# A fused retention and ELU kernel on one core: closing retention outputs pair by pair, loading two chunks earlier, and one multiply on VectorE instead of GpSimd

## The chip, the core and the metric

The kernel runs on one core of a Trainium2 chip. The core has TensorE for matmuls (PE in the profile, with its weight loads as PEld), VectorE (DVE), ScalarE (ACT), GpSimd (POOL), and SyncE (SP), which issues all of this kernel's DMAs in one queue. The metric is the device time of one execution in microseconds (us); lower is better. Everything is float32.

## What is computed

A recurrent retention block feeds a two-layer network. Sizes: batch 4, 8 heads, 768 tokens, head size 64; then 3072 tokens of 512 features, 2048 hidden features, 512 outputs.

```python
# retention: q, k, v are (B, H, S, D) = (4, 8, 768, 64)
gamma = 1.0 - 2.0 ** (-5.0 - np.arange(H))
for t in range(S):
    state = gamma[None, :, None, None] * state + np.einsum('bhd,bhe->bhde', k[:, :, t], v[:, :, t])
    y[:, :, t] = (1 / np.sqrt(D)) * np.einsum('bhd,bhde->bhe', q[:, :, t], state)
x = y.transpose(0, 2, 1, 3).reshape(B * S, H * D)      # (3072, 512)
# network with ELU: w_in is (512, 2048), w_out is (2048, 512)
h = x @ w_in
g = np.where(h > 0.0, h, np.exp(np.minimum(h, 0.0)) - 1.0)
out = g @ w_out
```

## The kernel before

**Tiling.** The 3072 tokens are 24 chunks of 128, numbered 0 to 23, and six groups of 512 tokens (four chunks, `CPB`), numbered `tb` 0 to 5 in the code and called the first to the sixth group in the text. A chunk's q, k and v arrive as one DMA of 1 MB (`load`, L113) into a tile `chunk` of `ldpool`. That pool has four buffers, so chunk m takes the buffer that chunk m - 4 had, and its DMA waits until that chunk is no longer read. After landing, its v is multiplied by powers of gamma (`scale_v`, L293), by GpSimd unless VectorE is asked for.

**Retention of a group** runs on chunks in two pairs (`pp` 0 and 1):
- `scores`: small 64x64 matmuls (L319) into `sc`, masked by VectorE (L330).
- `states`: small matmuls (L359) into `kv`, summed to states by VectorE (L371) or copied by ScalarE (L369).
- `outputs`: a generator for one pair. Its first part does the matmuls inside a chunk (`within`, L415) into two tiles `y` and stops. The second does half of the matmuls with the states (`across`, L430), has VectorE copy a corner of each `y` (`seen`, L399) and stops. The third does the other half of `across`, which waits for the `seen` copies, and then VectorE multiplies both `y` by decay powers into the group's input x (L405). Below, "closing" a pair is this third part. Each pair holds two of the four buffers of the pool `ps_r`.

`outputs_step` spreads this over three visits. In the kernel before, visit 0 starts pair 0, visit 1 starts pair 1, and visit 2 closes both. Between visits TensorE has other matmuls. The first group has its outputs written out by hand and does not use `outputs_step`.

**Network.** Both products are done by Strassen-like schemes with seven products in place of eight, some two levels deep. The first group's first product is plain (`plain_first`, L518 and L542), and its ELU is ScalarE's two steps (L498, L499) and VectorE's L502. While it runs, weights are decoded: ScalarE at L171 to L175, VectorE at L197, L198 and L201. The second product of the second group is `second_twice` (L924): seven outer products `j` in the order 1, 2, 6, 7, 5, 3, 4, each of seven inner products. Each inner product reads one 256 KB weight tile `wq` that SyncE fetches from `scratch_dram` (L830). There are 11 buffers for these, and a fetch is issued in the order of a list as soon as a product gives a buffer back. The first products of the later groups are `big_twice` (L1152), their second products L1248. From the third group on, two groups are done together.

**Order.** The schedule is by hand: generators are advanced step by step, and each engine runs its instructions in the order in which the code issues them. `step` counts the outer products of `second_twice`, and `VISITS` and `LOADS` are tables from a place in that count to a visit or a load. In the kernel before, the third group's visits 0 to 2 are before `step` 1 ends, and the fourth group's four loads follow:

```python
step, VISITS = 0, {(1, "first"): 3, (1, "end"): 4}
LOADS = {(1, "first"): 0, (2, "end"): 1, (5, "end"): 2, (6, "middle"): 3}
```

`retention_step(2, 3)` is visit 1 of the third group and `retention_step(2, 4)` is visit 2. `(1, "first")` is after the first two inner products of the second outer product, `(1, "end")` after its fifth. The fourth group's `scores` begin when `second_twice` ends; its visits lie in the first two products of `big_twice`.

The second group's `scale_v` calls are in the loop over `plain_first`; `n` counts its steps:

```python
if n in (3, 5, 7, 9):
    scale_v(CPB + (n - 3) // 2)
```

Of the kernel before, what the change touches and what calls it, by code (L numbers as in the profile page):

```python
# [19 lines left out]
def kernel(  # L20
# [46 lines left out]
    CPB = TB // C  # L67
# [34 lines left out]
    def load(m, cuts=(0, 2048), behind=None):  # L102

        if m >= NCHUNK:
            return
        t = ldpool.tile([P, 2048], FP32, name="chunk", tag="chunk")
        raw[m] = (
            t[:, 0:1024].rearrange("p (a h c) -> p a h c", a=2, c=C),
            t[:, 1024:2048].rearrange("p (a h d) -> p a h d", a=2, d=D),
        )  # L110
        hold(t, behind)
        for lo, hi in itertools.pairwise(cuts):
            nc.sync.dma_start(t[:, lo:hi], qkv[m, :, lo:hi])  # L113
# [171 lines left out]
    held = {}  # L285

    def scale_v(m, by_vector=False):
        if m >= NCHUNK:
            return
        i = chunks[m][1]  # L290
        v = raw[m][1][:, 0]
        eng = nc.vector if by_vector or m < 2 else nc.gpsimd
        eng.tensor_tensor(  # L293
            out=v, in0=v, in1=vf[:, i].unsqueeze(2).to_broadcast([C, H, D]), op=ALU.mult
        )
# [77 lines left out]
    def states(tb, pp):  # L373

        kvs = [ps_r.tile([P, 2, HP, D], FP32, name="kv", tag="r") for _ in range(2)]
        for x in range(2):
            state_products(kvs, tb, pp, x, range(2))
        for x in range(2):
            for sub in range(2):
                state_sum(kvs, tb, pp, x, sub)  # L380
# [4 lines left out]
    def outputs(tb, pp):  # L385

        y = [ps_r.tile([P, 2 * 2, 2, D], FP32, name="y", tag="r") for _ in range(2)]
        for x in range(2):
            for j in range(4):
                pt = raw[tb * CPB + 2 * pp + j // 2][0][:, 1].rearrange("p h c -> p (h c)")  # L390
                within(tb, pp, x, j, y, lambda p: pt[:, (x * HP + p) * D :][:, 0:D])
        for other in range(2):
            if not other:
                yield
            else:

                for sub in range(2):
                    seen = epool.tile([P, 8], FP32, name="seen", tag="seen")
                    nc.vector.tensor_copy(seen.rearrange("p (j x) -> p j x", x=2), y[sub][:, :, :, 0])  # L399
                yield  # L400
            for x in range(2):
                across(tb, pp, x, other, y)
        i = chunks[tb * CPB + 2 * pp][1]
        for sub in range(2):
            nc.vector.tensor_tensor(  # L405
                out=place_of(x_of(tb)[:, :, 2 * pp * C : 2 * (pp + 1) * C])[:, :, :, sub, :], in0=y[sub],
                in1=place_of(powers[:, :, i * C : (i + 2) * C])[:, :, :, sub, :], op=ALU.mult,
            )

    def within(tb, pp, x, j, y, pt):  # L410
        kv = raw[tb * CPB + 2 * pp + x][1]
        a, u = divmod(j, 2)
        for sub in range(2):
            for c in range(2):
                nc.tensor.matmul(  # L415
                    y[sub][rows(c), j, x, :], lhsT=kv[rows(sub), 0, head(a, u, c), :], rhs=pt(2 * u + c)[rows(sub)],
                    start=(x == 0 and j == 0), stop=False, skip_group_check=True,
                )

    def across(tb, pp, x, other, y):  # L420
        q = raw[tb * CPB + 2 * pp + x][0]
        for u in range(2):
            for a in range(2):
                sub = a ^ other
                n = 4 * pp + 2 * x + sub
                if fresh(tb, n):
                    continue
                for c in range(2):
                    p = 2 * u + c
                    nc.tensor.matmul(  # L430
                        y[sub][rows(c), 2 * a + u, x, :], lhsT=state(tb, n)[rows(a), p, :],
                        rhs=q[rows(a), 0, p, rows(sub)], start=False, stop=True, skip_group_check=True,
                    )

    def outputs_of_first():

        y = [bank(x).rearrange("p a (b x d) -> p (a b) x d", b=2, x=2) for x in "bd"]
        for x in range(2):
            for j in range(4):
                pt = raw[x][0][:, 1].rearrange("p h c -> p (h c)")  # L440
                within(0, 0, x, j, y, lambda p: pt[:, ((j // 2) * HP + p) * D :][:, 0:D])
            yield
            across(0, 0, x, 0, y)
            for sub in range(2):
                if not fresh(0, 2 * x + sub):
                    seen = epool.tile([P, 8], FP32, name="seen", tag="seen")
                    nc.vector.tensor_copy(seen[:, 0:4], y[sub][:, :, x, 0])
            if x:
                yield
            across(0, 0, x, 1, y)  # L450
            if x:
                yield
            for sub in range(2):
                nc.vector.tensor_tensor(
                    out=place_of(xb[:, :, 0 : 2 * C])[:, :, x, sub, :], in0=y[sub][:, :, x],
                    in1=place_of(powers[:, :, 0 : 2 * C])[:, :, x, sub, :], op=ALU.mult,
                )
            if not x:
                yield

    def outputs_step(tb, step):

        if step == 0:
            held["y"] = [outputs(tb, pp) for pp in range(2)]
        if step < 2:
            next(held["y"][step])
            next(held["y"][step])
        else:
            for g in held["y"]:
                next(g, None)  # L470

    half = [slice(0, TH), slice(TH, TB)]

# [83 lines left out]
    def inputs_of_first(f, slots):  # L557

        b11, b12, b21, b22 = (of_first(r, f, t) for r in range(2) for t in range(2))
        t3, t2, t4_ = slots  # L560
        tt = lambda o, x, y: nc.vector.tensor_tensor(out=o, in0=x, in1=y, op=ALU.subtract)
        tt(t3, b22, b12)
        tt(b12, b12, b11)
        yield
        tt(t2, b22, b12)
        tt(t4_, b21, t2)
        for x in range(2):
            inputs[f + x] = {
                1: of_first(0, f + x, 0, 1), 2: of_first(1, f + x, 0, 1), 3: of_first(1, f + x, 1, 1),
                4: t4_[:, x], 5: of_first(0, f + x, 1, 1), 6: t2[:, x], 7: t3[:, x],  # L570
            }
        yield
# [831 lines left out]
    y = outputs_of_first()  # L1404
# [40 lines left out]
    y = outputs(0, 1)  # L1445
# [9 lines left out]
    def run(steps):  # L1455
        for _ in steps:
            pass

    def next_piece(by_vector=False):
        decode_all()  # L1460
        prepare(by_vector=by_vector)
# [8 lines left out]
    for n, _ in enumerate(inner):  # L1470
        if n in (0, 2, 4):
            load(CPB + n // 2)
        if n == 4:
            load(CPB + 3)
        if n in (1, 2, 4, 5, 7, 9):
            next_piece(n in (1, 2, 5, 7))
        if n in (3, 5, 7, 9):
            scale_v(CPB + (n - 3) // 2)
        if n == 4:
            run(inputs_of_first(0, [hslot() for _ in range(3)]))  # L1480
        elif n == 10:
            scores(1, 0)
            scores(1, 1)
        elif n == 11:
            states(1, 0)
            states(1, 1)
            next_piece()
            parts = sums_of_pieces(0)
            next(parts)
        elif n == 12:  # L1490
            outputs_step(1, 0)
            run(parts)
            next_piece()
        elif n == 13:
            outputs_step(1, 1)
            smalls = small_of_pieces(0)
            some(smalls, 3)
        elif n == 14:
            outputs_step(1, 2)
            some(smalls, 2)  # L1500
            decode_all()
        elif n == 15:
            run(smalls)
# [114 lines left out]
    flush()  # L1618
    retention_step(2, 2)
    step, VISITS = 0, {(1, "first"): 3, (1, "end"): 4}  # L1620
    LOADS = {(1, "first"): 0, (2, "end"): 1, (5, "end"): 2, (6, "middle"): 3}
    for s in sec:
        if s == "first":
            step += 1
# [1 line left out]
        if at in VISITS:  # L1626
            retention_step(2, VISITS[at])
        if at in LOADS:
            load(3 * CPB + LOADS[at])
            scale_v(3 * CPB + LOADS[at])  # L1630
        if s == ORDER2[-1]:
# [10 lines left out]
    for nb in range(NB):  # L1642
# [173 lines left out]
        step = 0  # L1816
# [3 lines left out]
        ]  # L1820
        LOADS = [(3, "middle"), (3, "end"), (4, "first"), (4, "middle")]
        for s in sec:
# [4 lines left out]
            if more and at in VISITS:  # L1827
                n = VISITS.index(at)
                retention_step(groups[n // 5], n % 5)
            if more and at in LOADS:  # L1830
                bring(groups[1], LOADS.index(at))
            if s == BIG2[-1]:
# [56 lines left out]
```

## Time and profile before

| what | value |
|---|---|
| runs | 621.24 us median of 3 (621.15 to 623.93) |
| profiled execution | span 621.4 us, from its first to its last instruction; the profile shows no time outside it |
| TensorE | 611.4 us busy (98%), granted clock 1.000 |
| VectorE | 496.7 us busy (80%) |
| ScalarE | 261.0 us busy (42%) |
| GpSimd | 21.2 us busy (3%) |
| DMA | 125.14 MB, mean 201 GB/s |

The table gives the median of the runs and the profile of one execution. "Busy" is the union of an engine's instructions. Matmuls are pipelined and their recorded ends are modelled, so the distance between two starts tells more of TensorE than an instruction's length. In a row of the timeline, the numbers are the start, the length, the engine, the line, the operation, the tiles (out<-in), the shape and the count; a bracket at the end gives the idle time before it and what ended it. "issue" means that the engine waited for nothing that the profile shows. `SPq` is SyncE's queue. In a row of waits the numbers are the total, the times and the longest. In a row by stretches they are the stretch and its length, the busy time and instructions of PE, PEld, DVE, ACT and POOL, the granted clock, the share of DMA and its GB/s.

### The profile page before, as it was taken

How to read it: one execution, taken by the hardware profiler on the slowest of the kernel's cores; microseconds unless marked ns; L12 is line 12 of the kernel's file. 1: busy time of each engine (PE TensorE's matmuls, PEld its weight loads, DVE VectorE, ACT ScalarE, POOL GpSimd, SP SyncE). 2: the span in 40 equal slices, each digit the busy share in tenths (PEclk: the TensorE clock that was granted, in tenths of full speed). 3: DMA queues.
4: the chain of work that ended last, by engine and by line, in shares of the span. 5: the costliest groups of instructions: out<-in, count | busy, mean ns of one | idle time of the engine just before them, and what ended most of it. 6: DMA issues, size and time to landing. Idle time of an engine off the chain costs nothing.

```text
span 621.4 us, 13415 instructions
## 1 busy us (share of the span) xinstructions
PE 611.4 (98%) x5446; PEld 480.9 (77%) x5446; DVE 496.7 (80%) x776; ACT 261.0 (42%) x446; POOL 21.2 (3%) x30
## 2 busy tenths in 40 slices
PE   8999999999999999999999999999999999999998
PEld 6764568888889998888545888888888744788886
DVE  5768889989889875677888987898546897888885
ACT  5888844205542111236898210100144798511110
POOL 2011000000000001000010000110000000000000
PEclk9999999999999999999999999999999999999999
DMA  8697569789575898786811445873654523356453
GB/s 295 285 374 303 174 205 269 235 242 274 204 234 151 301 374 310 231 250 199 274 49 67 122 134 154 268 275 108 206 159 143 151 69 93 118 148 187 153 150 117
DMA packets 79278, 125.14 MB, mean 201 GB/s; under 512 B 6128, under 2 KB 46832, under 8 KB 74480
## 3 DMA queue, kind: packets, MB, share of 16 engines
q1 hardware_dynamic: 79216, 124.28, 62.1%
q8 instruction: 43, 0.70, 0.4%
q14 instruction: 19, 0.16, 0.1%
HBM read 94.63 MB, written 29.62 MB: 200 GB/s over the span
## 4 chain that ended last, share of the span: by engine, by line
PE 86%; DVE 4%; DMA 3%; ACT 3%; issue 2%; SPq 0%; DVEq 0%
PE pa L1248 15%; PE pa L1152 9%; PE pd L1248 8%; PE pa L1199 6%; PE pd L1152 4%; PE pa L765 4%; PE pd L1199 4%; PE pb L1248 4%; PE x L632 3%; DMA wq<-scratch_dram 2%; PE pa L924 2%; PE pa L542 2%; PE pb L1152 2%; PE pa L632 2%; PE pb L1199 2%; PE y L415 2%
## 5 line engine op out<-in xcount | busy, mean ns | idle before, releaser
L1256 ACT COPY ms<-pa 128x256 f32<-128x256 f32 x41 | 15.3, 372 | 108.5 <-PE pa L1248 105.5
L1248 PE MATMUL pa<-gC,wq 128*128 128x256 f32 x224 | 53.1, 381 | 0.0
L1248 PEld LDWEIGHTS pa<-gC,wq 128*128 128x128 f32 x224 | 42.1, 190 | 6.8 <-DVE gT L1216 0.5
L1215 ACT ACTIVATE r<-r 128x512 f32<-128x512 f32 x64 | 40.3, 630 | 2.0
L1163 ACT COPY m<-pa 128x512 f32<-128x512 f32 x32 | 18.7, 585 | 48.9 <-PE pa L1152 48.8
L293 POOL TENSOR_TENSOR chunk<-chunk,vf 128x512 f32<-128x512 f32 x16 | 18.0, 1124 | 381.3 <-DMA chunk<-in_qkv_dram 201.1
L1260 DVE TENSOR_TENSOR res<-pd,ms 128x256 f32<-128x256 f32 x26 | 11.0, 422 | 25.0 <-PE pd L1248 14.1
L1152 PE MATMUL pa<-ts,wq 128*128 128x256 f32 x104 | 26.9, 384 | 0.0
L1248 PE MATMUL pa<-ts,wq 128*128 128x256 f32 x112 | 26.8, 382 | 0.0
L1248 PE MATMUL pd<-w_all,wq 128*128 128x256 f32 x112 | 26.6, 380 | 0.1
L171 ACT ACTIVATE w_all<-wraw 128x1024 uint32<-128x1024 uint32 (+1 forms) x19 | 19.2, 1008 | 16.9 <-PE x L632 9.0
L1248 PE MATMUL pd<-ts,wq 128*128 128x256 f32 x104 | 24.7, 380 | 0.2 <-DVE ts L894 0.2
L1230 DVE TENSOR_TENSOR gC<-w_all,gC 128x1024 f32<-128x1024 f32 x20 | 24.2, 1260 | 0.0
L1248 PEld LDWEIGHTS pd<-w_all,wq 128*128 128x128 f32 x112 | 21.2, 190 | 3.4 <-DVE w_all L894 0.6
L1248 PEld LDWEIGHTS pa<-ts,wq 128*128 128x128 f32 x112 | 21.0, 190 | 2.9
L1248 PE MATMUL pa<-w_all,wq 128*128 128x256 f32 x96 | 22.9, 381 | 0.0
L173 ACT ACTIVATE w_all<-wraw 128x1024 fp8e4<-128x1024 f32 (+1 forms) x19 | 22.6, 1189 | 0.6
L1152 PEld LDWEIGHTS pa<-ts,wq 128*128 128x128 f32 x104 | 19.3, 190 | 4.5 <-ACT m L1163 0.8
L1216 DVE SCALAR_TENSOR_TENSOR w_all<-r,w_all 128x512 f32<-128x512 f32 x32 | 22.0, 688 | 0.7 <-ACT r L1215 0.6
L1248 PEld LDWEIGHTS pd<-ts,wq 128*128 128x128 f32 x104 | 19.7, 190 | 3.2 <-DVE ts L894 0.6
L1199 PE MATMUL pa<-ts,wq 128*128 128x512 f32 x48 | 22.1, 592 | 0.0
L1199 PE MATMUL pa<-gC,w_all 128*128 128x512 f32 x48 | 22.1, 592 | 0.0
(327 smaller groups left out, 1458.0 us busy)
## 6 DMA issues: line engine op xcount, KB each, us to landing
wq<-scratch_dram SPq DMA_DIRECT2D x191, 256.0 KB, 3.2
chunk<-in_qkv_dram SPq DMA_DIRECT2D x22, 1024.0 KB, 7.6
wraw<-in_w_dram SPq DMA_DIRECT2D x15, 1024.0 KB, 7.1
out_dram<-res SPq DMA_DIRECT2D x7, 512.0 KB, 3.3
scratch_dram<-gT SPq DMA_DIRECT2D x12, 256.0 KB, 4.3
wq<-scratch_dram SPq DMA_DIRECT2D x24, 128.0 KB, 3.1
scratch_dram<-w_all SPq DMA_DIRECT2D x12, 256.0 KB, 3.4
scratch_dram<-w_all SPq DMA_DIRECT2D x24, 128.0 KB, 3.2
```

Source lines behind the costliest of these rows:

```text
L171: nc.scalar.activation(flat, lo, AF.Copy, scale=2.0**-29)
L173: nc.scalar.activation(top, hi.bitcast(FP32), AF.Copy, scale=2.0**-120, saturate=False)
L293: eng.tensor_tensor(out=v, in0=v, in1=vf[:, i].unsqueeze(2).to_broadcast([C, H, D]), op=ALU.mult)
L632: nc.tensor.matmul(X[j][:, d, :], lhsT=w[j][:, d * P : d * P + P], rhs=x[j], start=(n == 0 and d == 0), stop=at_end, skip_group_check=True,)
L765: nc.tensor.matmul(ps[:, fi, :], lhsT=w[:, fi, j2, :], rhs=x[:, j2, :], start=(begin and fi == 0 and j2 == 0), stop=(j2 == 1), skip_group_ ...
L1152: nc.tensor.matmul(ps[:, f, :], lhsT=w[:, f, :], rhs=big_xs[j][k], start=(begin and f == 0), stop=True, skip_group_check=True,)
L1163: nc.scalar.copy(o, ps)
L1199: nc.tensor.matmul(ps, lhsT=w[:, k, :], rhs=layer_x[j][:, k], start=False, stop=(k == 1), skip_group_check=True,)
L1215: nc.scalar.activation(r, r, AF.Exp, scale=-1.0)
L1216: return lambda: nc.vector.scalar_tensor_tensor(g, r, -1.0, g, ALU.add, ALU.max)
L1230: nc.vector.tensor_tensor(out=quarter(to, r, t), in0=quarter(x, r, t), in1=quarter(y, r, t), op=op)
L1248: nc.tensor.matmul(ps, lhsT=w[:, f, :], rhs=ts[j][k][:, f // 2, f % 2, :], start=(begin and f == 0), stop=(f == 3), skip_group_check=True,)
```

## The change

Three edits:
- In `outputs_step`, groups with `tb` up to 3 close pair 0 at the head of visit 1, and pair 1 at visit 2. Groups 4 and 5 close both at visit 2, as before. Since group 0 does not come here, groups 1, 2 and 3 change.
- The v of chunk 6 is multiplied by VectorE at step `n` = 8 of `plain_first`, not by GpSimd at step 7.
- The third and the fourth load of the fourth group (chunks 14 and 15) are issued one place sooner each in the count: at `(4, "end")` and `(5, "end")`.

```diff
         if step == 0:
             held["y"] = [outputs(tb, pp) for pp in range(2)]
+        early_end = tb <= 3
+        if step and early_end:
+            next(held["y"][step - 1], None)
+        elif step == 2:
+            for g in held["y"]:
+                next(g, None)
         if step < 2:
             next(held["y"][step])
             next(held["y"][step])
-        else:
-            for g in held["y"]:
-                next(g, None)
...
-        if n in (3, 5, 7, 9):
+        if n == 8:
+            scale_v(CPB + 2, True)
+        if n in (3, 5, 9):
             scale_v(CPB + (n - 3) // 2)
...
-    LOADS = {(1, "first"): 0, (2, "end"): 1, (5, "end"): 2, (6, "middle"): 3}
+    LOADS = {(1, "first"): 0, (2, "end"): 1, (4, "end"): 2, (5, "end"): 3}
```

On the engines, by the order of instructions: TensorE has the same matmuls, with pair 0's closing ones ahead of pair 1's first. On VectorE two L405 move ahead of the second pair's two `seen` copies in each of the three groups, and one L293 is added between the L502 of `pb` and that of `pd`. GpSimd has 15 L293 in place of 16. ScalarE's order does not change. On SyncE chunk 14 comes four `wq`, one output and three `wq` earlier, and chunk 15 three `wq` and one output earlier.

## The prediction

> **What bounds the kernel now.** I read the page first (busy shares, then the chain that ended last), then TensorE's waits, then the timeline around each wait.
>
> ```profile
> PE 611.4 (98%) x5446; PEld 480.9 (77%) x5446; DVE 496.7 (80%) x776; ACT 261.0 (42%) x446; POOL 21.2 (3%) x30
> PE 86%; DVE 4%; DMA 3%; ACT 3%; issue 2%; SPq 0%; DVEq 0%
> q8 instruction: 43, 0.70, 0.4%
> ```
>
> TensorE is busy 98% of the span and carries 86% of the chain, at a granted clock of 1.0 throughout. The change adds and removes no matmul, so it can only pay or cost where TensorE stands still. Those places, from the waits of TensorE:
>
> ```profile
> PE pa L924 <- DMA wq<-scratch_dram: 1.3, 1, 1.3
> PE sc L319 <- issue: 0.6, 1, 0.6
> PE y L415 <- issue: 0.8, 2, 0.5
> PE pa L542 <- DVE gC L502: 0.4, 1, 0.4
> ```
>
> Four holes lie near the edits: 0.4 us at L542 (group one's tail, where one v changes engine), 1.3 us at L924 (group two's second product, while the fourth group's chunks load), and two "issue" holes, at L319 and at the second of the two L415 waits (fourth group's retention). The timeline, by start and length, shows each hole and its neighbour:
>
> ```profile
> 49.05 3.60 PE L542 MATMUL pd<-xb,w_all 128*128 128x512 f32 x8
> 53.05 1.13 PE L542 MATMUL pa<-xb,w_all 128*128 128x512 f32 x2 [0.40 <-DVE gC L502]
> ...
> 218.71 1.06 PE L924 MATMUL pd<-ts,wq 128*128 128x128 f32 x8
> 221.02 1.13 PE L924 MATMUL pa<-ts,wq 128*128 128x128 f32 x8 [1.25 <-DMA wq<-scratch_dram]
> ...
> 245.14 1.04 PE L319 MATMUL sc<-chunk 64*64 64x64 f32 x55
> 246.79 0.35 PE L319 MATMUL sc<-chunk 64*64 64x64 f32 x9 [0.62 <-issue]
> 246.96 1.26 PE L359 MATMUL kv<-chunk 64*64 64x64 f32 x64
> ```
>
> Ends of matmuls are modelled, so I price a hole from start to start against an undisturbed group of the same kind. L542: eight take 3.43 (45.62 to 49.05), here 49.05 to 53.05 is 4.00: 0.57 us. L924: eight take 0.89 (217.82 to 218.71), here 2.31: 1.42 us. L319: 64 small matmuls take 0.98 (191.68 to 192.66), here 245.14 to 246.96 is 1.82: 0.84 us. L415: 250.07 to 251.56 is 1.49 against 0.98: 0.51 us. Together 3.34 us. Nothing else within reach of the edits stands still by more than 0.22 us (L924 at 190.59), so a gain over about 3.6 us is excluded.
>
> **One v on VectorE.** The release of L542 at 53.05 leads to VectorE, and from there to GpSimd:
>
> ```profile
> 50.27 1.04 POOL L293 TENSOR_TENSOR chunk<-chunk,vf 128x512 f32<-128x512 f32 x1 [3.89 <-DMA chunk<-in_qkv_dram]
> ...
> 50.35 2.05 DVE L201 CUSTOM_DVE_ANT_0 w_all<-wraw,w_all 128x2048 uint16<-128x2048 uint16 x1
> 52.32 1.27 DVE L502 SCALAR_TENSOR_TENSOR gC<-r,pa 128x512 f32<-128x512 f32 x2
> ...
> 54.96 1.23 DVE L201 CUSTOM_DVE_ANT_0 w_all<-wraw,w_all 128x2048 uint16<-128x2048 uint16 x1
> ...
> 58.70 0.69 DVE L502 SCALAR_TENSOR_TENSOR gC<-r,pd 128x512 f32<-128x512 f32 x1 [1.92 <-ACT r L499]
> ```
>
> The same L201 takes 1.23 us alone and 2.05 beside GpSimd's multiply: 0.82 lost, which is what makes L502, and so L542, late. It is chunk 6 that is scaled at 50.27; that is the one moved. L201 then ends near 51.6, the r it waits for is there (ScalarE ends it at 51.51), the first L502 ends near 52.2, before the 52.48 at which TensorE could start. Gain 0.57. The multiply itself goes between the L502 of pb and that of pd, where VectorE idles 1.92 us; a two-input 128x512 operation there takes 0.69 (L561, 48.42). It is hidden; without that cover it costs at most 0.69. The chunk landed by 50.3, so VectorE does not wait on it. GpSimd's next multiply (52.58) waits for its own chunk anyway.
>
> The Trainium skill ("Perfetto Trace Analysis", section "Optimizing Scalar/DVE Operations") says the reverse of this edit: where VectorE is saturated, move work off it, even to GpSimd; though it warns in the same place that the two share a port. The stretch agrees with the warning (2.05 against 1.23); by the first half alone this term would be a loss, the fourth case below.
>
> **Outputs pair by pair.** Group one does not go through this routine, so groups two to four change. In each, the 32 closing matmuls of pair 0 (as the trace counts them) move from the third visit to the head of the second. Visits stay three per group, so the price of switching between big and small matmuls stays: zero on TensorE. A switch shows as 0.10 us (193.24 to 194.23, right after small matmuls, against 0.89), so 0.2 up or down per group bounds it. On VectorE two of the four L405 (four take 2.48 at 204.15, so 0.62 each) move ahead of the two "seen" copies, which pair 1's closing matmuls wait for. Group three: seen now starts at 199.67, would end near 201.2, and is wanted at 202.33: 1.1 us spare. In groups two and four VectorE idles before the same copies (0.70 at 78.19, 1.92 at 256.61). Should that cover be gone, up to 1.3 us per group; I take 0.
>
> The use is elsewhere. Load 12 takes the buffer of chunk 8, last read by pair 0's closing matmuls. SyncE issues in order, and stood behind that wait:
>
> ```profile
> SPq L113 <- PE y L430: 4.9, 1, 4.9
> ...
> 201.00:205.00 4.00, 4.00 (x91) 3.81 (x90) 3.06 (x7) 0.53 (x2) 0.00 (x0) 1.00 0.23 43
> 222.00:230.00 8.00, 8.00 (x74) 8.00 (x73) 5.32 (x11) 1.32 (x5) 0.00 (x0) 1.00 1.04 378
> ```
>
> (First the wait in SyncE's queue; then stretches, whose last two columns are DMA share and GB/s.) From 198.4 to 203.1 SyncE issued nothing: DMA fell to 43 GB/s, then had chunk 12, the waiting wq and chunk 13 at once and ran full until past 230. The hole at 221 is a wq that SyncE issued at 213.80, behind chunk 13. Now pair 0 closes near 198.5, so load 12 and the wq behind it go 4.6 us sooner. Full rate 378 GB/s less what the products draw (262 KB per 0.89 us, 294) leaves 84 GB/s to catch up. Serving 4.6 us sooner is 1.7 MB at full rate; the hole of 1.42 us is 0.5 MB. Gain 1.42, bounds 0 and 1.42.
>
> **Two loads sooner.** Chunks 14 and 15 move from 231.25 and 236.29 to about 223.5 and 230. In SyncE's queue they pass four wq, an output and three wq, and then three wq and an output: each passed issue is 0.4 us later, and about 2.8 us behind a chunk's megabyte (1.05 MB at 378). A wq is issued when one of 11 buffers comes free, so 11 x 0.89 = 9.8 us before use; usual landing is 5.5 us in this stretch. The spare 4.3 us covers 2.8. Their buffers (chunks 10 and 11) are long free; GpSimd multiplies both sooner, with nothing queued behind. Cost 0.
>
> What it gives: chunk 15 no longer fills DMA in 236 to 244 (349 GB/s in 236 to 242, 285 in 242 to 250). The "issue" hole stands in the middle of 64 equal matmuls with no semaphore, and small matmuls eat instructions fastest (64 of them with their 64 weight loads in 0.98 us); I read it as instructions arriving late through busy DMA engines. Gain 0.84, bounds 0 and 0.84. The L415 hole follows 4 us later, when scratch stores fill DMA, and those stay: I take 0, bounds 0 and 0.51. In return, fetches near 199 to 203 now meet chunk 12: 0, up to 0.84 by the nearest row.
>
> The Trainium skill ("Runtime: NRT & Kernel Launch", section "Instruction fetch mechanics") tells of instructions streamed in 16 KiB blocks of 256, mostly hidden. The page's row agrees on the size (0.70 MB in 43); by "mostly hidden" the hole has another cause and stays, the third case.
>
> **Sum.** Profiled execution: span 621.4, nothing shown around it, 0.2 above the median of 621.24, so I subtract from the median: 0.57 + 1.42 + 0.84 = 2.83, 618.4 us.
>
> **Cases.** 0.5% of 621.24 is 3.1 us (about what a measurement of this kernel can tell from no change), so the faster side begins at 618.1.
> 1. Three holes close, the L415 one stays: 618.4. Chance 0.38.
> 2. All four close: 621.24 - 3.34 = 617.9. For it: with 0.6 us gained just before, TensorE reaches this L415 earlier against the stores. Chance 0.32.
> 3. Both "issue" holes stay, since they come from how dense the small matmuls are: 621.24 - 1.99 = 619.25. For it: a like hole at 25.4, long before these loads. Against: dense stretches at 60 and 171 have none. Chance 0.10.
> 4. The v is in VectorE's way: + 0.69 - 1.42 - 0.84, 619.7. Against: the 1.92 idle. Chance 0.05.
> 5. The wq hole only moves, and only the v helps: 620.7. Chance 0.06.
> 6. Slower: the two loads come before the backlog is served. Catching up one chunk at 84 GB/s takes 12.5 us, and chunks now stand 11.5, 13.5 and 6.5 us apart. If wq land over 9.8 us after issue from 223 on, each load stalls TensorE its 2.8 us and no DMA hole closes: 621.24 - 0.57 + 5.6 = 626.3. Against: the 6.5 us follow only after most of this product's wq are issued. Chance 0.09.
>
> Faster by over 0.5%: most of case 2 and, 618.4 being 0.3 from the edge, under half of case 1: 0.45. Within: 0.46. Slower: case 6, 0.09. The range leaves out case 6 and reaches from 617.3 (case 2, the 0.22 at 190.59 and 0.4 of switches) to 620.9.
>
> **What would show it.** L201 near 50 takes 1.23 and no idle stands before L542; an L293 on DVE lies between two L502. SyncE's wait on L430 falls under 1 us, DMA in 201 to 205 is busy, no L924 waits for wq. L319 of the fourth group runs its 64 unbroken. I am wrong if L924 or L1152 waits for wq after 223, if L430 waits for "seen", or if a new "issue" hole appears near 200.

## The result and the profile after

| kernel | median (lowest to highest), us | runs | span of the profiled execution |
|---|---|---|---|
| before | 622.67 (620.76 to 624.97) | 22 | 621.4 |
| changed | 620.52 (619.32 to 623.74) | 22 | 618.6 |

The changed kernel takes 0.9973 of the time of before, with a 95% interval of 0.9961 to 0.9985: 0.27% faster, which on 622.67 is 1.7 us (0.9 to 2.4). The medians lie 2.15 apart, the means of the same runs 1.8. Single runs of either kernel scatter with a standard deviation of 1.1 to 1.2 us, so three runs, as the prediction had them, or one profile, say little about 1.7 us.

The page after, rows of its first and fourth parts:

```profile
PE 610.7 (99%) x5446; PEld 481.2 (78%) x5446; DVE 494.7 (80%) x777; ACT 261.0 (42%) x446; POOL 22.1 (4%) x29
PE 89%; DMA 5%; DVE 3%; ACT 1%; SPq 1%; issue 1%; DVEq 0%
```

The matmuls are the same 5446, and their share of the chain grew from 86 to 89%: TensorE does the same work and stands still less. VectorE has one instruction more and GpSimd one less, as the edit says.

TensorE's waits after; the three numbers are the total, the times and the longest:

```profile
PE y L415 <- issue: 0.6, 1, 0.6
PE pd L430 <- DVE seen L447: 0.5, 2, 0.3
PE pa L927 <- DMA wq<-scratch_dram: 0.3, 1, 0.3
PE y L430 <- DVE seen L399: 0.3, 1, 0.3
```

From line 471 on, three lines were added, so the L924 of before is L927 here, L542 is L545 and L502 is L505. Of the four holes that the prediction priced, three are gone, and the `wq` one is down from 1.3 to 0.3. The "issue" wait that is left is the one of the start (at 25.46), which before had too. The waits for `seen` stand as they were, so closing pair 0 early cost nothing here.

The two rows of the fourth group's retention that were broken by an "issue" wait before (L319 at 246.79, L415 at 251.26) run their 64 matmuls through:

```profile
243.27 1.16 PE L319 MATMUL sc<-chunk 64*64 64x64 f32 x64
...
247.32 1.16 PE L415 MATMUL y<-chunk 64*64 64x64 f32 x64
```

SyncE's queue in before, at load 12:

```profile
203.09 0.33 SPq L113 DMA_DIRECT2D chunk<-in_qkv_dram  x1
203.47 4.14 SPq L830 DMA_DIRECT2D wq<-scratch_dram  x7
```

The queue after (its wait on L430, then its timeline), and the stretch in which before had moved 43 GB/s with the next one (the last two columns are DMA share and GB/s):

```profile
SPq L113 <- PE y L430: 0.6, 2, 0.3
```

```profile
197.77 0.33 SPq L113 DMA_DIRECT2D chunk<-in_qkv_dram  x1
200.23 6.50 SPq L833 DMA_DIRECT2D wq<-scratch_dram  x7
207.53 0.34 SPq L968 DMA_DIRECT2D out_dram<-res  x1
207.96 1.81 SPq L833 DMA_DIRECT2D wq<-scratch_dram  x3
209.82 0.42 SPq L113 DMA_DIRECT2D chunk<-in_qkv_dram  x1
```

```profile
201.00:205.00 4.00, 4.00 (x63) 3.81 (x63) 3.78 (x8) 0.53 (x2) 0.00 (x0) 1.00 0.93 347
205.00:213.00 8.00, 8.00 (x74) 8.00 (x73) 4.46 (x11) 1.32 (x5) 1.04 (x1) 1.00 0.82 254
```

The wait of 4.9 us is gone. Load 12 goes out at 197.77 in place of 203.09. The seven `wq` behind it begin at 200.23 in place of 203.47. TensorE is 0.9 us further on in this profile, so the load gains 4.4 us and the `wq` 2.4; the prediction gave 4.6 to both. The quiet stretch runs at 347 GB/s.

VectorE and GpSimd around 50 us after, by start and length:

```profile
50.14 1.23 DVE L201 CUSTOM_DVE_ANT_0 w_all<-wraw,w_all 128x2048 uint16<-128x2048 uint16 x1
50.72 1.55 POOL L293 TENSOR_TENSOR chunk<-chunk,vf 128x512 f32<-128x512 f32 x1 [6.42 <-DMA chunk<-in_qkv_dram]
51.29 1.27 DVE L505 SCALAR_TENSOR_TENSOR gC<-r,pa 128x512 f32<-128x512 f32 x2
...
55.08 0.68 DVE L505 SCALAR_TENSOR_TENSOR gC<-r,pb 128x512 f32<-128x512 f32 x1
...
55.68 0.68 DVE L293 TENSOR_TENSOR chunk<-chunk,vf 128x512 f32<-128x512 f32 x1
```

L201 takes its 1.23 as forecast, and the moved multiply takes 0.68 in VectorE's idle time. But GpSimd still multiplies beside an L201. This is now chunk 7's multiply, whose chunk landed at 50.56, and GpSimd is the one that takes longer, 1.55 in place of 1.04. What decides is in the experiments.

### The profile page after: what moved, and what is told of

Same layout as the page of the kernel before. It is cut to its first block, busy times and chain, and to the rows that moved or that the text cites. A ratio compares the mean times of both kernels' runs of the same rounds, so it can differ in the third digit from the quotient of the medians.

```text
span 618.6 us, 13412 instructions
## 1 busy us (share of the span) xinstructions
PE 610.7 (99%) x5446; PEld 481.2 (78%) x5446; DVE 494.7 (80%) x777; ACT 261.0 (42%) x446; POOL 22.1 (4%) x29
## 4 chain that ended last, share of the span: by engine, by line
PE 89%; DMA 5%; DVE 3%; ACT 1%; SPq 1%; issue 1%; DVEq 0%
PE pa L1251 15%; PE pa L1155 9%; PE pd L1251 8%; PE pa L1202 6%; PE pd L1155 4%; PE pd L1202 4%; PE pb L1251 4%; PE pa L545 3%; PE x L635 3%; DMA wq<-scratch_dram 3%; PE pa L768 3%; PE pa L927 3%; PE pb L1155 2%; PE pa L635 2%; PE pb L1202 2%; PE y L415 2%
## 5 line engine op out<-in xcount | busy, mean ns | idle before, releaser
L293 POOL TENSOR_TENSOR chunk<-chunk,vf 128x512 f32<-128x512 f32 x15 | 19.0, 1265 | 377.2 <-DMA chunk<-in_qkv_dram 201.2
```

The source lines that it names most:

```text
L293: eng.tensor_tensor(out=v, in0=v, in1=vf[:, i].unsqueeze(2).to_broadcast([C, H, D]), op=ALU.mult)
```

## The experiments

**The theories.** T1: the prediction's own, the v gives 0.57, the earlier closing 1.42, the two loads 0.84. T2: some of these holes differ from execution to execution, and a part of the 3.34 us belongs to the one profile shown and not to the kernel. To see that, before and the changed kernel were profiled again as well. Each ratio is against runs of before on the same chip.

**The v alone.**

```diff
-        if n in (3, 5, 7, 9):
+        if n == 8:
+            scale_v(CPB + 2, True)
+        if n in (3, 5, 9):
             scale_v(CPB + (n - 3) // 2)
```

> The kernel before with one edit: chunk 6's v goes to VectorE. Theory A (each edit closes its own hole, and hole sizes are the same in every execution): L201 near 50 takes 1.23 us, the 0.57 us at L542 is gone, the wq hole near 221 stays at about 1.4 us and both issue holes stay; time 0.6 us under before (ratio 0.9991). Theory B (the holes that hang on DMA differ from one execution to the next, and the profile of before was one large draw): the L542 hole is gone in the same way, since nothing of it hangs on DMA, and the time is also 0.6 under before, but the wq hole and the issue holes in this profile have other sizes than 1.42, 0.84 and 0.51. Theory C (the v is in VectorE's way): 0.7 us slower.

Measured: 622.18, ratio 1.0002 (0.998 to 1.0025). The v alone gives nothing that 12 runs show. The interval reaches to a gain of 1.2 us, so for the 0.57 this does not decide alone; the profiles below do.

The trace shows a cost that the prediction had not looked for, behind the last matmul. From its start to the end of the span it is 3.93 us here, and 3.46 to 3.47 in the four profiles of before. The first of GpSimd's two `DRAIN` instructions at the end of the program starts 3.29 us after that matmul in place of 2.96, and takes 0.22 in place of 0.08; the last instructions of all engines come later by as much. All seven profiles of kernels with this v on VectorE have 3.93 to 3.96 there, and all seven with it on GpSimd 3.46 or 3.47. So the edit costs 0.49 us at the end. Why GpSimd is late there is not shown.

**The closing alone.**

```diff
+        early_end = tb <= 3
+        if step and early_end:
+            next(held["y"][step - 1], None)
+        elif step == 2:
+            for g in held["y"]:
+                next(g, None)
```

> The kernel before with one edit: pair 0 closes at the head of the second visit in groups two to four. Theory A: SyncE's wait on L430 is under 1 us, the wq hole near 221 closes (1.42 us), the L542 hole and the issue holes stay: 1.4 us under before (0.9977). Theory B: the wq hole is smaller but not surely gone; the mean gain is under 1.4 us, between 0.3 and 1.2. A rival (the visits themselves cost): switches or seen waits show on L430, time equal or slower.

Measured: 621.62, ratio 0.998 (0.9963 to 0.9998). Load 12's wait on L430 is 0.3, TensorE waits for no `wq`, and by chance this execution shows what the v was about. VectorE and GpSimd in it:

```profile
49.79 1.04 POOL L293 TENSOR_TENSOR chunk<-chunk,vf 128x512 f32<-128x512 f32 x1 [4.99 <-DMA chunk<-in_qkv_dram]
49.91 1.47 DVE L198 TENSOR_SCALAR wraw<-wraw 128x1024 uint32<-128x1024 uint32 x1
51.42 1.23 DVE L201 CUSTOM_DVE_ANT_0 w_all<-wraw,w_all 128x2048 uint16<-128x2048 uint16 x1
```

GpSimd began first, and VectorE's L198, 0.70 elsewhere, took 1.47; TensorE then stood 0.50 us longer at L545.

**The loads alone.**

```diff
-    LOADS = {(1, "first"): 0, (2, "end"): 1, (5, "end"): 2, (6, "middle"): 3}
+    LOADS = {(1, "first"): 0, (2, "end"): 1, (4, "end"): 2, (5, "end"): 3}
```

> The kernel before with one edit: chunks 14 and 15 are loaded one place sooner each. SyncE still stands 4.9 us behind load 12. Theory A: the wq hole near 221 stays at 1.4 us; the issue hole at L319 closes (0.84 us), the one at L415 closes too (0.51, as in the profile of the changed kernel): 0.8 to 1.35 us under before (0.9978 to 0.9987). Theory B: the same holes, with a mean gain under that. A rival (loads before the backlog is served): new wq holes at L924 near 225 to 232, up to 2.8 us per load, time slower by up to 5.6 us.

Measured: 621.04, ratio 0.9969 (0.9955 to 0.9983), the clearest single gain. No "issue" hole at L319 or L415 is left. SyncE's wait is still 4.9 us, and the `wq` holes are still there:

```profile
213.85 1.13 PE L924 MATMUL pd<-ts,wq 128*128 128x128 f32 x8 [0.65 <-DMA wq<-scratch_dram]
...
220.96 1.13 PE L924 MATMUL pa<-ts,wq 128*128 128x128 f32 x8 [1.51 <-DMA wq<-scratch_dram]
```

After 223, where the sixth case of the prediction had put its stalls, nothing waits for a `wq`.

**Before again.** No edit.

> The kernel before, unchanged. Theory A: its profile shows the four holes with the sizes of the first profile: 0.57, 1.42, 0.84 and 0.51 us, span 621.4. Theory B: 0.57 again to within 0.05, but the wq hole and the issue holes differ by half a microsecond or more, and the span with them (the runs of before reach from 620.8 to 625.0 us). The ratio to before is 1.000 either way and shows how far a comparison of this many rounds can be trusted.

Measured: 622.65, ratio 0.9998 (0.9982 to 1.0014). Its profile of the same kernel has other holes. VectorE and GpSimd in it:

```profile
49.91 1.24 DVE L201 CUSTOM_DVE_ANT_0 w_all<-wraw,w_all 128x2048 uint16<-128x2048 uint16 x1
50.18 1.86 POOL L293 TENSOR_TENSOR chunk<-chunk,vf 128x512 f32<-128x512 f32 x1 [3.51 <-DMA chunk<-in_qkv_dram]
```

In the profile shown to the prediction GpSimd began at 50.27 and VectorE 0.08 us later; here VectorE began 0.27 us ahead. Whichever begins first keeps its time, the other waits: 1.86 for GpSimd here, 2.05 for VectorE there. The Trainium skill ("SBUF — State Buffer", section "SBUF: two separate sides") states this as a rule: the two share a port pair, and the one that starts first holds it for the whole instruction. These rows agree.

The fourth group's small matmuls in the same profile (TensorE's timeline):

```profile
243.95 1.04 PE L319 MATMUL sc<-chunk 64*64 64x64 f32 x55
245.86 0.35 PE L319 MATMUL sc<-chunk 64*64 64x64 f32 x9 [0.88 <-issue]
246.03 1.26 PE L359 MATMUL kv<-chunk 64*64 64x64 f32 x64
247.22 1.13 PE L1152 MATMUL pa<-xt,w_all 128*128 128x256 f32 x4
248.19 1.03 PE L1152 MATMUL pd<-ts,w_all 128*128 128x256 f32 x4
249.15 0.92 PE L415 MATMUL y<-chunk 64*64 64x64 f32 x46
250.88 0.50 PE L415 MATMUL y<-chunk 64*64 64x64 f32 x18 [0.81 <-issue]
```

The break comes after the 55th matmul of L319, as in the first profile of before, and then after the 46th of L415, again as there. From the first break to the second there are 9 + 64 + 4 + 4 + 46 = 127 matmuls, as many weight loads and, in the trace, two semaphore instructions: 256. This holds for every "issue" wait of TensorE. The 14 profiles of this document show 18, of 0.17 to 0.88 us, and counted from the start of the program each comes after 193 or 194 instructions more than a multiple of 256. The Trainium skill ("Runtime: NRT & Kernel Launch", section "Instruction fetch mechanics") has instructions come in blocks of 256. The trace agrees.

The trace also has the packets of the instruction queue, `q8`: 43 of 16 KB in each profile, as many as there are such places. The first packet comes after the first place, so I pair each packet with the place after (the trace does not name what a packet holds). Then no place in any of the 14 profiles is passed less than 1.25 us after its packet has ended, and all 18 holes end 1.25 to 1.51 us after it. So at these holes TensorE waits for instructions that arrive late.

**The closing and the loads, v on GpSimd.** The changed kernel with this undone:

```diff
-        if n == 8:
-            scale_v(CPB + 2, True)
-        if n in (3, 5, 9):
+        if n in (3, 5, 7, 9):
             scale_v(CPB + (n - 3) // 2)
```

> The changed kernel with chunk 6's v given back to GpSimd. Theory A (v is worth 0.57 us in every execution): 0.6 us slower than the changed kernel, ratio to before 0.9982. Theory B' (GpSimd and VectorE take turns at a shared port, and whichever starts first goes through; the 0.57 us came up only because GpSimd started 0.08 us before L201 in that one execution): no measurable difference from the changed kernel, ratio near 0.997; in the profile the later one of L293 and L201 is the long one.

Measured: 620.48, ratio 0.9975 (0.9959 to 0.9991). On the same chip the changed kernel has 0.9972. The v is worth nothing that shows.

**The changed kernel again.** No edit.

> The changed kernel, unchanged. If holes have fixed sizes (theory A): span 618.6 again, a wq hole of 0.44 us near 219, no issue hole at L319 or L415, ratio to before 0.9955. If one profile is a single draw (theory B): the wq hole and the start-up differ by up to 1 us and the span with them, and the ratio is again near 0.997.

Measured: 620.35, ratio 0.9972 (0.9954 to 0.999), on another chip, beside 0.9973 in the first comparison. None of the four holes is in its profile (span 617.7).

**Chunk 13's load later.** The changed kernel, with

```diff
-    LOADS = {(1, "first"): 0, (2, "end"): 1, (4, "end"): 2, (5, "end"): 3}
+    LOADS = {(1, "first"): 0, (3, "first"): 1, (4, "end"): 2, (5, "end"): 3}
```

> The changed kernel with chunk 13's load moved from the end of the second step to the first place of the third, about 3 us later. If the wq hole near 219 is made by wq that stand behind chunk 13: it closes (0.44 us in the profile of the changed kernel), ratio to before near 0.996. Rival (the backlog is what counts, not the place): a hole of 0.5 to 1.5 us at L924 shows 2 to 4 us later, near 222 to 226, and the ratio is 0.997 to 0.999.

Measured: 619.66 (619.0 to 620.5), ratio 0.9966 (0.9954 to 0.9978), the lowest median of all kernels. In the first profile of the changed kernel the `wq` issued right behind load 13, at 210.34, landed at 219.02, and the 0.3 us hole that is left ends at 219.16. Here load 13 goes out at 212.51 in place of 209.82, more `wq` pass it, and TensorE stands still for none. It is faster than before; from the changed kernel on the same chip (620.35) its interval does not separate it.

**Pair by pair in all groups.** The changed kernel, with

```diff
-        early_end = tb <= 3
+        early_end = True
```

> The changed kernel with pair 0 closed early in the fifth and sixth groups too. Their outputs lie between 366 and 445, where no hole over 0.15 us stands in TensorE's timeline and DMA is under 300 GB/s. Theory A and B alike: nothing to gain, ratio as the changed kernel, 0.997. Rival: the early L405 delay VectorE there and a wait on ts or res shows at L1251 (0.3 to 1.3 us), ratio near 0.999.

Measured: 624.17, ratio 1.0041 (1.0023 to 1.0059): slower than before. TensorE's waits, and then the timeline where the longest of them falls:

```profile
PE y L430 <- DVE seen L399: 2.7, 3, 2.0
```

```profile
375.47 1.23 DVE L897 TENSOR_TENSOR gC<-gC,gC 128x1024 f32<-128x1024 f32 x1
376.61 0.23 DVE L399 COPY seen<-y 128x8 f32<-128x8 f32 x2
...
376.90 0.27 PE L430 MATMUL y<-chunk 64*64 64x64 f32 x2 [2.00 <-DVE seen L399]
```

Closing pair 0 one visit sooner also needs its `seen` copy one visit sooner. In the fifth group that copy is queued on VectorE behind additions over 1024 columns (L897), and TensorE stands for 2.0 us; a second hole, 0.44, follows at 433.37. Start to start the two cost 2.16 and 0.60. This is the wait that the prediction named for L430, priced at up to 1.3 per group; where VectorE is full it is larger. In groups two to four it did not come. The profiled execution (622.25) is the fastest of this kernel's twelve runs, so the others lose more than these two holes; where is not shown.

**Pair by pair in the third group alone.** The changed kernel, with

```diff
-        early_end = tb <= 3
+        early_end = tb == 2
```

> The changed kernel with the early closing kept in the third group alone (the one whose chunk 8 load 12 waits for); groups two and four close both pairs at the third visit again. If all that the early closing brings is load 12: the same as the changed kernel, ratio near 0.997, SyncE's wait on L430 under 1 us, no wq hole over 0.5 us. Rival (the earlier L405 in groups two and four matter as well): ratio nearer 1.000, and a wait on L405 or a y buffer shows in TensorE's timeline near 83 to 87 or 256 to 260.

Measured: 620.91, ratio 0.9977 (0.9961 to 0.9992): not to be told from the changed kernel. The second and fourth groups add nothing that shows. Its profile holds a miss for the theory. SyncE's wait is 0.3 here too, and yet (TensorE's timeline):

```profile
220.40 1.13 PE L927 MATMUL pa<-ts,wq 128*128 128x128 f32 x8 [1.74 <-DMA wq<-scratch_dram]
```

**Three more profiles**, one execution each: two of before and one of the changed kernel, to see how the holes scatter.

> The kernel before, for its profile alone. Holes of fixed size: 0.57, 1.42, 0.84 and 0.51 us. Holes that differ by execution: the L542 hole is there only if GpSimd's L293 starts before VectorE's L201; the wq hole lies between 1.0 and 1.7, the L319 hole between 0 and 1.1, the L415 hole between 0.4 and 1.1.

> As the run before it: the kernel before, a further execution. The sum of the four holes over all profiles of this kernel, less what the changed kernel keeps, should come near the 1.7 us that the runs show, not the 2.8 of the first pair of profiles.

> The changed kernel, for its profile alone: wq hole between 0 and 1 us, no L542 hole, no issue hole at L319, at most 0.5 us at L415.

Measured: 622.75 and 622.66 for before, 620.70 for the changed kernel. In us that TensorE loses, start to start as in the prediction, a hole being the time over that of an undisturbed group:

| profile | L542 (v) | `wq` | L319 | L415 | sum |
|---|---|---|---|---|---|
| before, as predicted from | 0.57 | 1.42 | 0.84 | 0.51 | 3.34 |
| before, second | 0 | 1.21 | 1.09 | 1.03 | 3.33 |
| before, third | 0 | 1.80 | 0.28 | 0 | 2.08 |
| before, fourth | 0 | 1.52 | 0.54 | 1.03 | 3.09 |
| v alone | 0 | 1.48 | 0 | 0.49 | 1.97 |
| closing alone | 0.50 | 0 | 0 | 0.41 | 0.91 |
| loads alone | 0 | 2.50 | 0 | 0 | 2.50 |
| changed, first | 0 | 0.44 | 0 | 0 | 0.44 |
| changed, second | 0 | 0 | 0 | 0 | 0 |
| changed, third | 0 | 0.64 | 0 | 0 | 0.64 |
| closing and loads | 0 | 0.40 | 0 | 0 | 0.40 |
| load 13 later | 0 | 0 | 0 | 0 | 0 |
| all groups | 0 | 0 | 0 | 0 | 0 |
| third group alone | 0 | 1.90 | 0 | 0 | 1.90 |

(All groups has its two holes at L430 beside these.) The third profile of the changed kernel has a new hole as well:

```profile
203.24 0.60 PE L927 MATMUL pa<-gC,wq 128*128 128x128 f32 x4 [0.34 <-issue]
```

It is the "issue" hole near 200 that the prediction had allowed for, 0.51 start to start; it shows in one of three profiles of the changed kernel, and it too stands at a place of the 256.

## Why the prediction was right or wrong

**Direction and range held, the size did not.** Forecast was 618.4, in a range of 617.3 to 620.9; measured is 620.52. The three terms made 2.83 us; the runs give 1.7 (0.9 to 2.4). Faster, but within 0.5%.

**The v: the term that failed.** The prediction gave it a gain of 0.57 and no cost. The 0.57 was a price from one execution. In it GpSimd began 0.08 us ahead of VectorE. In the other three profiles of before VectorE began first, GpSimd waited, and TensorE lost nothing. A hole that comes in one profile of four is worth 0.14 on average (0.15 over all seven profiles with this v on GpSimd, two of which have it). The prediction took from the row that the multiply slows L201, and did not ask which of the two comes first in another execution. The multiply itself was hidden, as said, and the fourth case, in which it costs 0.69 in VectorE's way, did not come. But the premise that the change "can only pay or cost where TensorE stands still" left out what follows the last matmul, and there the edit costs 0.49. By the profiles the term is thus a loss of about 0.35 in place of a gain of 0.57. The runs (1.0002, and 0.9975 against 0.9972) show neither; their intervals are wider than that.

**The closing: right, at its upper bound.** SyncE's longest wait on L430 at a load went from 4.9 to 0.3 or less in each of the eight profiles of kernels that close the third group's pair 0 early. In the six profiles that close late the `wq` holes sum to 1.2 or more, 1.66 on average. In the eight that close early the average is 0.42, and four of those have none. So the term of 1.42 measured 1.2. It is a lower chance of a hole and not its end: 0.44 and 0.64 in two profiles of the changed kernel, and 1.90 in the one with the third group alone. "Gain 1.42" was the upper bound taken as the value. Cost 0 held in the groups that were changed, and the fifth and sixth, which were left out, show what it is without cover.

**The loads: right, and more than priced.** In the six profiles with the loads late (four of before, v alone, closing alone) the L319 hole is there four times and the L415 hole five times; in the eight with the loads early neither is ever there. The sum took L319 at 0.84, and L415 at 0 since the scratch stores stay. On average before loses 0.69 at L319 and 0.64 at L415, and both go: that step was too careful, and it was the second case that came. That the holes come from instructions that arrive late is shown by their places and by the packets. With the loads late, the packet ended 1.25 to 1.51 us before TensorE passed the place in eleven of the twelve cases (six profiles, L319 and L415); with the loads early, 1.66 to 2.27 us before in all sixteen. What differs between the two is when chunk 15 lands. In the six profiles it was still landing 1.45 to 2.60 us after TensorE had passed the place before L319's; in the eight it had landed at least 0.86 us before that. The twelfth case, 2.19 at L319 with the closing alone, shows that a packet can come through beside the load, so that the load's bytes hold the packet up is likely but not shown. The third case is out, in which these holes come from how dense the small matmuls are: they reach 0.88 us of idle time, and they go when two loads move. The Trainium skill ("Runtime: NRT & Kernel Launch", section "Instruction fetch mechanics") calls the cost of a new block mostly hidden. In 584 of the 602 places of these 14 traces no wait shows, which agrees; the 18 waits do not.

**The base: wrong.** "Nothing shown around it, 0.2 above the median" set a span beside a run's time. The profiled execution of the changed kernel has a span of 618.6 and took 620.36, and the second one of before 621.7 and 623.47: some 1.8 us lie outside the span, in every run for which both are on record (1.72 to 1.85). The profiled execution of before thus took about 623.2 (an estimate, 621.4 + 1.8), and the 621.24 from which the sum was subtracted was 1.4 below the median of 22 runs. From 622.67, the two terms that held, 1.42 + 0.84, give 620.4. That this is 0.1 from the measured 620.52 is partly luck, since the closing was priced too large, and what was left out goes both ways: 0.64 at L415, the 0.49 at the end, and the new hole.

**The slower case** had the loads stall the `wq` after 223. No profile with the loads early has that.

**The sum again, and what stays open.** By the table before loses 2.96 us on average in four profiles, and the changed kernel 0.53 (with its new hole) in three: 2.4 us. Less the 0.49 at the end this is 1.9, beside the 1.7 (0.9 to 2.4) of the runs. The spans say 2.85 (621.25 against 618.4, means of four and three). Of that, 0.57 lies between the span's start and TensorE's 641st matmul, where no edit has acted yet: this stretch took between 36.25 and 38.38 us in the 14 profiles, in part by a wait of L347 for the first chunks that is 0 to 1.2 us. So spans of a few profiles carry scatter that no edit made. Open is how the gain divides: 0.31% for the loads alone (0.17 to 0.45) and 0.20% for the closing alone (0.02 to 0.37) do not add up to 0.27 or 0.28% for the whole, but the intervals allow it. Open too are the 1.90 us hole of the third group alone and the 0.49 at the end.

## What to carry to other kernels

A hole of under 1 us in one profile is one draw: before it goes into a sum at full size, ask which two things race to make it (which of two engines starts first, which transfer lands first), and price it by its share of several executions. An engine's wait inside a queue that issues all DMAs costs what stands behind it; look at the quiet stretch of DMA and at the crowded one after it, not only at the transfer that waits. A busy engine's holes are not all that an edit can change: compare the stretch after its last instruction too. When closing work is moved one visit sooner, the small copy that it depends on is due one visit sooner as well, and what decides is what is queued ahead of that copy.

## What was not expected of the hardware

- The TensorE "issue" holes stand at fixed places of the instruction stream, multiples of 256 instructions apart, while their lengths differ from execution to execution: at L319, 0.84, 1.09, 0.28 and 0.54 in four profiles of the same kernel. Each ends 1.25 to 1.51 us after a packet of the instruction queue.
- A multiply on GpSimd takes 1.04 when it begins first and up to 1.95 when VectorE does (at 36.93 in the v alone); it slows L198 (0.70 to 1.47) as well as L201 (1.23 to 2.05).
- With chunk 6's multiply on VectorE the end of the program takes 0.49 us longer, in seven profiles of seven.
- With SyncE's queue no longer held, DMA still falls off between 205 and 213, to 254 GB/s, with `wq` outstanding; the stretch after it moves 381. Why was not found. The 1.90 us hole of the third group alone follows such a stretch (263 GB/s), but the second profile of the changed kernel has one too (266) and no hole.
